# Packed attention, gated MLP and routed attention, eight sequences: keys and queries turned head by head between matrix products, GpSimd joins the planes, last queries' scores block-diagonal

## The chip, the cores and the metric

One core of a Trainium2 chip runs the whole program. The metric is device time in microseconds (us) of one execution, the median of several. "TensorE" is PE (PEld is its weight load), "VectorE" DVE, "ScalarE" ACT, "GpSimd" POOL; SyncE (SP) only issues DMAs.

## What is computed

For each of 8 sequences (b = 0 to 7) of 576 tokens, three layers follow one another:

```
p_packed = softmax(p k^T / 8) v                 # 8 heads of 64, 32 packed queries per head
x        = softmax(q p_packed^T / 8) p_packed   # back to 576 tokens, 512 wide
h = gelu(x w_in);  u, v = halves of h;  v = layernorm(v) * g
x = x + (u * (w_sg v + b_sg)) w_out             # mixing over tokens
# four experts, each a causal attention over the whole sequence with a head of 64
out = sum over the two best experts e of gate_e(x) * softmax(x wq_e (x wk_e)^T / 8, causal) x wv_e wo_e
```

Products are float32; most are made from a high and a low part of each operand in three passes (`PASSES`).

## The kernel before

**Stages of a sequence.** TensorE's order is written out by hand (`manual_schedule`). `startup` prepares the weights (w_in and w_out arrive as float64 bit patterns and are rebuilt on VectorE) and does sequence 0 as far as its gated product; its last steps load `moe2_wo` into `wst` (`prep_w_o`, L311) and split it into `w_o`. Then comes `back(0)`, and for b = 1 to 7 `front(b)` and `back(b)`. `front` makes the v part of the MLP (`v_tiles`) and the u part (`u_tile`). `back` mixes the tokens (`vs_tile`), makes the per-head products `bdq` and `bdv` (`bdw`), then queries, keys, values and gate logits of the experts (`qk`, `vlog`, `gates`). Between these stand the expert attention of sequence b-1 (steps S, T, y, o: scores and softmax, transposes, product with the values, output) and the packed attention of sequence b+1. A **loop** below is the time from the start of `v_tiles` of one sequence to that of the next.

**Keys and queries of the packed attention** need the 64 head dims on partitions. From sequence 1 on, a DMA does that, on 16-bit halves. `turn` (L386) transposes two heads at once from the input into an SBUF tile `x` (two buffers), and writes the tile to a scratch tensor in DRAM (`turned_k`, `turned_q`). `planes` (L393) reads it back so that low and high half-words of a number stand in separate planes (`kp`, `qp`), and `join` (L399) interleaves the planes into float32 (`kT`, `qT`): plane 0 is copied on GpSimd, plane 1 on ScalarE. Step K joins keys (K0 two pairs of heads, K1 two) and loads query planes, Q joins queries; s0 and s1 are the scores of the packed queries with the keys (L436), a0 and a1 transpose the softmax (L463, from the exponentials of L445), p and P make the packed values, r the second softmax. Step f, in `back` after the last `vs_tile`, loads the key planes of the next sequence and half of its values.

**The last queries.** Tokens 512 to 575 are a tile of 64 rows. For a pair of experts, `att_last` (L884; steps S8 and S9) makes 12 products of 64x64 by 288 into two PSUM tiles, one per expert (L896), adds the mask (L902), takes the maximum (L903) and the exponential (L904) of each, and scales both (L905 to L907). PSUM has four tiles (`pd`).

**Order.** Only TensorE's order is the program's. For ACT, DVE, POOL and SP a list scheduler with a model of times sets the order; each engine then executes in order, and SP issues its DMAs in order, each with its own waits (buffers, data). `ahead(b)` adds the load of p and the eight turns for sequence b; `startup` calls `ahead(1)`, and `back(b)` calls `ahead(b+2)`. kept_qk, kept_vg, kept_in are weights rearranged in DRAM, of which `load_w` brings w_qk, w_vg and the halves of w_in each time into two buffers (tag W).

Of the kernel before, what the change touches and what calls it, by code (L numbers as in the profile page):

```python
# [7 lines left out]
F32 = mybir.dt.float32  # L8
# [9 lines left out]
P = 128  # L18
# [8 lines left out]
def packed_attention_mlp_moe_kernel(  # L27
# [37 lines left out]
    BY = {"A": 1152, "B": 576, "C": 640, "D": 576, "a": 1152, "p": 576, "T": 512, "x": 576, "t": 576, "W": 2048}  # L65
# [33 lines left out]
    for i in range(E):  # L99
        for j in range(E):  # L100
            nc.vector.memset(tri[:, i, j:j + 1], 1.0 if j < i else 0.0)
    mhalf = consts.tile([P, 1], F32, name="mhalf")
# [219 lines left out]
    def load_nat(name, src, b, j):  # L322
# [6 lines left out]
        elif (b, name) == (0, "k") and j >= 2:  # L329
            t = slot("x", w=512, name=name)  # L330
        else:
            t = nat_slot(F32, name)
# [27 lines left out]
    STEP = {}  # L360

    def p1_steps(b):
# [23 lines left out]
        def turn(name, src, j):  # L386
            x = sb.tile([P, 2, S], U16, tag="x", name=name + "x", bufs=NB["x"])
            rows = src[b, 2 * j:2 * j + 2].rearrange("h s d -> (h s) d").bitcast(U16)
            nc.sync.dma_start_transpose(x.rearrange("p h s -> p (h s)"), rows)
            s[name + "x", j] = dram.tile([P, 2, S], U16, name=f"turned_{name}{b}{j}")  # L390
            nc.sync.dma_start(s[name + "x", j], x)
# [7 lines left out]
        def join(name, j):  # L399
# [3 lines left out]
            nc.gpsimd.tensor_copy(w[:, 0], t[:, 0].rearrange("p h n -> p (h n)"))  # L403
            act_copy(w[:, 1], t[:, 1].rearrange("p h n -> p (h n)"))
# [141 lines left out]

        for name, src in (("k", k), ("q", q)):
            for j in range(4):
                add(0, turn, name, src, j)
# [249 lines left out]

    def vlog(b, cs):  # L800
# [83 lines left out]
    def att_last(b, pr):  # L884

        s = ST[b]
        qs, ks = s["qk", pr], s["qk", 2 + pr]
        at = slot("B" if b + 1 == B else "a", w=S, name="at")
        st = small.tile([P, 2, 2], F32, name="st3")
        sm = small.tile([P, 2], F32, name="sm4")  # L890
        pts = [pd("sc") for _ in range(2)]
        for i, (x, y) in enumerate(PASSES):
            for h in range(2):
                for e in range(2):
                    r = slice(64 * e, 64 * e + 64)
                    nc.tensor.matmul(pts[e][:64, h, :HALF], qs[x][r, 4 * P:S], ks[y][r, hs(h)],  # L896
                                     start=i == 0, stop=i == 2)
        for e in range(2):
            r = slice(64 * e, 64 * e + 64)
            se = st[:64, e, :]  # L900
            d = pts[e][:64, 1, HALF - 64:HALF]
            nc.vector.tensor_tensor(d, d, causal[:64, :64], op=OP.add)  # L902
# [331 lines left out]
```

## Time and profile before

| | |
|---|---|
| Median of 3 runs | 960.96 us (960.46 to 961.58) |
| The profiled execution | 959.91 us, span 958.2 us (1.7 us lie outside) |
| PE busy | 839.3 us (88% of the span), 7613 products |
| DVE, ACT, POOL busy | 581.2, 477.2, 128.2 us |
| DMA | 114.09 MB, mean 119 GB/s |
| v_tiles of sequences 1, 2, 3, 7 start at | 202.8, 327.6, 428.4, 830.4 us |

How to read it: the engines run side by side, so a busy time counts only where something waits for it. A matmul's end is modelled. "[19.96 <-ACT u]" behind a row is the idle time of that engine before the instruction, and what ended it by the profile; where the named engine had long been done, it was something else, often a DMA. The chain that ended last is PE for 60% of the span, DMA for 9% and ACT for 6%.

### The profile page before, as it was taken

How to read it: one execution, taken by the hardware profiler on the slowest of the kernel's cores; microseconds unless marked ns; L12 is line 12 of the kernel's file. 1: busy time of each engine (PE TensorE's matmuls, PEld its weight loads, DVE VectorE, ACT ScalarE, POOL GpSimd, SP SyncE). 2: the span in 40 equal slices, each digit the busy share in tenths (PEclk: the TensorE clock that was granted, in tenths of full speed). 3: DMA queues.
4: the chain of work that ended last, by engine and by line, in shares of the span. 5: the costliest groups of instructions: out<-in, count | busy, mean ns of one | idle time of the engine just before them, and what ended most of it. 6: DMA issues, size and time to landing. Idle time of an engine off the chain costs nothing.

```text
span 958.2 us, 19292 instructions
## 1 busy us (share of the span) xinstructions
PE 839.3 (88%) x7613; PEld 701.8 (73%) x7613; DVE 581.2 (61%) x1419; ACT 477.2 (50%) x1061; POOL 128.2 (13%) x148
## 2 busy tenths in 40 slices
PE   4687634799577999899999999999999999999987
PEld 2457523688456897789878887888788877898965
DVE  7669241386333876478647765586548665876365
ACT  2445133265343566546563657275646565565345
POOL 0001030120011211021012101130112021210000
PEclk9898867899878999999999999999999999999989
DMA  9987889898794106320532144112422052200001
GB/s 302 249 216 172 196 236 254 207 197 203 213 260 104 68 1 201 85 72 3 169 94 56 43 134 116 45 68 72 151 71 67 25 172 64 68 1 35 12 7 50
DMA packets 168870, 114.09 MB, mean 119 GB/s; under 512 B 115594, under 2 KB 149642, under 8 KB 165964
## 3 DMA queue, kind: packets, MB, share of 16 engines
q1 hardware_dynamic: 168780, 112.86, 43.4%
q8 instruction: 60, 0.98, 0.4%
q14 instruction: 30, 0.25, 0.1%
HBM read 68.26 MB, written 29.63 MB: 102 GB/s over the span
## 4 chain that ended last, share of the span: by engine, by line
PE 60%; DMA 9%; ACT 6%; DVE 4%; issue 2%; SPq 1%; ACTq 0%
PE qk L774 9%; PE vs L729 8%; PE vlog L811 5%; PE qk L786 5%; PE v L661 4%; PE y L951 4%; PE u L711 4%; PE o L982 4%; PE sc L864 4%; PE vlog L815 3%; DMA qx<-in_q_dram 2%; PE aTp L922 2%; DMA turned_q<-qx 2%; DMA kx<-in_k_dram 2%; ACT at L904 1%
## 5 line engine op out<-in xcount | busy, mean ns | idle before, releaser
L774 PE MATMUL qk<-gh,w_qk 128*128 128x288 f32 x512 | 91.9, 302 | 2.2 <-ACT at L904 2.1
L729 PE MATMUL vs<-w_sg,vnh 128*128 128x288 f32 x512 | 92.8, 304 | 0.7 <-DVE w_sg L85 0.7
L774 PEld LDWEIGHTS qk<-gh,w_qk 128*128 128x128 f32 x512 | 75.2, 190 | 14.9 <-issue 7.2
L82 ACT ACTIVATE aT<-aTp 128x512 f32<-128x512 f32 (+4 forms) x160 | 60.5, 433 | 46.8 <-PE aTp L922 41.7
L877 ACT ACTIVATE at<-sc,nm 128x256 f32<-128x256 f32 (+3 forms) x128 | 66.4, 525 | 27.2 <-DVE nm L868 27.1
L729 PEld LDWEIGHTS vs<-w_sg,vnh 128*128 128x128 f32 x512 | 75.7, 191 | 5.3 <-issue 3.0
L982 PE MATMUL o<-w_o,y 128*128 128x512 f32 x192 | 55.8, 428 | 12.4 <-ACT pT L82 11.0
L811 PE MATMUL vlog<-w_vg,gh 128*128 128x260 f32 (+1 forms) x320 | 61.9, 291 | 0.0
L951 PE MATMUL y<-aT,v 128*64 128x128 f32 (+2 forms) x960 | 60.3, 265 | 0.8 <-ACT aT L82 0.8
L676 POOL TENSOR_TENSOR rstd<-rstd,mhalf 128x1 f32<-128x1 f32 x40 | 36.9, 929 | 164.4 <-DVE rstd L675 164.4
L951 PEld LDWEIGHTS y<-aT,v 128*64 128x64 f32 (+1 forms) x960 | 47.7, 138 | 13.9 <-issue 7.0
L774 PE MATMUL qk<-gl,w_qk 128*128 128x288 f32 x256 | 55.4, 298 | 1.9 <-DVE gl L85 1.9
L403 POOL COPY kT<-kp 128x576 uint16<-128x576 uint16 x28 | 24.8, 913 | 237.0 <-DMA kp<-turned_k 164.6
L729 PE MATMUL vs<-w_sg,vnl 128*128 128x288 f32 x256 | 55.4, 298 | 0.0
L868 DVE TENSOR_REDUCE nm<-sc 128x2 f32<-128x256 f32 (+3 forms) x64 | 52.6, 822 | 1.6
L881 DVE TENSOR_SCALAR at<-at,sm,gw 128x256 f32<-128x256 f32 (+3 forms) x128 | 51.4, 443 | 2.3
L982 PEld LDWEIGHTS o<-w_o,y 128*128 128x128 f32 x192 | 35.7, 200 | 23.3 <-ACT pT L82 11.2
L811 PEld LDWEIGHTS vlog<-w_vg,gh 128*128 128x128 f32 (+1 forms) x320 | 48.2, 180 | 3.5 <-issue 2.8
L864 PE MATMUL sc<-qk 64*128 64x256 f32 (+3 forms) x384 | 47.9, 356 | 0.0
L922 PE MATMUL aTp<-ident,at 128*128 128x128 f32 x320 | 47.8, 282 | 0.0
L786 PE MATMUL qk<-a2h,bdq 128*128 128x288 f32 x256 | 46.6, 303 | 0.2 <-DVE bdq L85 0.2
L878 DVE TENSOR_SCALAR sm<-sm 128x2 f32<-128x2 f32 x64 | 14.0, 218 | 52.5 <-ACT at L877 52.4
(208 smaller groups left out, 1947.7 us busy)
## 6 DMA issues: line engine op xcount, KB each, us to landing
w_in<-kept_in SPq DMA_DIRECT2D x14, 1024.0 KB
w_qk<-kept_qk SPq DMA_DIRECT2D x8, 1024.0 KB
out_dram<-ot SPq DMA_DIRECT2D x32, 256.0 KB
turned_k<-kx SPq DMA_DIRECT2D x28, 288.0 KB
turned_q<-qx SPq DMA_DIRECT2D x28, 288.0 KB
kp<-turned_k SPq DMA_DIRECT2D x56, 144.0 KB
qp<-turned_q SPq DMA_DIRECT2D x56, 144.0 KB
v<-in_v_dram SPq DMA_DIRECT2D x56, 128.0 KB
```

Source lines behind the costliest of these rows:

```text
L82: nc.scalar.activation(o, i, AF.Copy, scale=scale)
L729: nc.tensor.matmul(pt[:, h, :HALF], s["vn", c][x][:, cols], w_sg[y][:, c, hs(h)], start=(c, x, y) == (0, 0, 0), stop=False)
L774: nc.tensor.matmul(o[:, h, :], W["w_qk"][y][:, m, cols], s["g", m][x][:, hs(h)], start=first and (m, x, y) == (0, 0, 0), stop=not first an ...
L786: nc.tensor.matmul(o[:, h, :], s["bd", Q][y][:, cols], s["a2", Q][x][:, hs(h)], start=first and (Q, x, y) == (0, 0, 0), stop=not first and ...
L811: nc.tensor.matmul(pt[:n, ci, :260], s["g", m][x][:, c * P:c * P + n], W["w_vg"][y][:, m, :], start=(m, x, y) == (0, 0, 0), stop=False)
L864: nc.tensor.matmul(pt[:, e, :L], qs[x][r, j * P:L], ks[y][r, :L], start=i == 0, stop=i == 2)
L868: nc.vector.tensor_reduce(nm, pt[:, :, :L], axis=AX.X, op=OP.max, negate=True)
L877: nc.scalar.activation(ats[e][:, :L], pt[:, e, :L], AF.Exp, bias=nm[:, e:e + 1], accum_out=sm[:, e:e + 1])
L881: nc.vector.tensor_scalar(ats[e][:, :L], ats[e][:, :L], sm[:, e:e + 1], s["w"][:, j, 2 * pr + e:2 * pr + e + 1], op0=OP.mult, op1=OP.mult)
L922: nc.tensor.transpose(pt[:, e, c * P:c * P + P], ats[e][:, c * P:c * P + P], ident)
L951: nc.tensor.matmul(pt[64 * e:64 * e + 64, pr * w:pr * w + w], s["v2"][:m, c, col:col + D], s["aT", pr, e, j][c][:m, :], start=c == 0, stop ...
L982: nc.tensor.matmul(pt, ys[:, pr, x, :], W["w_o"][y][:, pr, :], start=i == 0, stop=i == 5)
```

## The change

- `turn` transposes one head, with one buffer of half the size; `keep` writes it to DRAM as a DMA of its own, in the next step. These steps stand in a list (`TURN`, 17 per sequence: 16 turns, each behind the `keep` of the head before, and a last `keep`). `tick` takes the next one: ten in `front(b)`, the rest before step f, six in `back(b)` for the sequence after; all 17 of sequence 1 at the end of `startup`.
- SP executes in program order from `back(0)` on.
- `join` makes both copies on GpSimd.
- `keep_last_q` copies the last 64 queries of a pair of experts (high and low part) into the diagonal blocks of a 128x128 tile of zeros, on GpSimd. `att_last` makes 6 products of 128x128 by 288 into one PSUM tile, and one maximum and one exponential over 128 partitions.
- S8 moves ahead of T6, S9 ahead of T7; step f ahead of "T5 S6 o1 T4".

```diff
@@ pools, constants, load_nat
-    BY = {"A": 1152, "B": 576, "C": 640, "D": 576, "a": 1152, "p": 576, "T": 512, "x": 576, "t": 576, "W": 2048}
+    BY = {"A": 1152, "B": 576, "C": 640, "D": 576, "a": 1152, "p": 576, "T": 512, "t": 576, "W": 2048}
+    last_q = [[consts.tile([P, P], F32R, name=f"last_q{i}{x}") for x in range(2)] for i in range(2)]
+    for z in last_q[0] + last_q[1]:
+        nc.gpsimd.memset(z.bitcast(F32), 0.0)
...
         elif (b, name) == (0, "k") and j >= 2:
-            t = slot("x", w=512, name=name)
+            t = slot("D", w=512, name=name)
@@ p1_steps
+    TURN = []
+
+    def tick(n=1):
+        for _ in range(min(n, len(TURN))):
+            for f in TURN.pop(0):
+                f()
...
-        def turn(name, src, j):
-            x = sb.tile([P, 2, S], U16, tag="x", name=name + "x", bufs=NB["x"])
-            rows = src[b, 2 * j:2 * j + 2].rearrange("h s d -> (h s) d").bitcast(U16)
-            nc.sync.dma_start_transpose(x.rearrange("p h s -> p (h s)"), rows)
-            s[name + "x", j] = dram.tile([P, 2, S], U16, name=f"turned_{name}{b}{j}")
-            nc.sync.dma_start(s[name + "x", j], x)
+        def turn(name, src, h):
+            x = sb.tile([P, S], U16, tag="x", name=name + "x", bufs=NB["x"])
+            nc.sync.dma_start_transpose(x, src[b, h].bitcast(U16))
+            if h % 2 == 0:
+                s[name + "x", h // 2] = dram.tile([P, 2, S], U16, name=f"turned_{name}{b}{h}")
+            s["x", name, h] = x
+
+        def keep(name, h):
+            nc.sync.dma_start(s[name + "x", h // 2][:, h % 2, :], s.pop(("x", name, h)))
...
-            nc.gpsimd.tensor_copy(w[:, 0], t[:, 0].rearrange("p h n -> p (h n)"))
-            act_copy(w[:, 1], t[:, 1].rearrange("p h n -> p (h n)"))
+            for i in range(2):
+                nc.gpsimd.tensor_copy(w[:, i], t[:, i].rearrange("p h n -> p (h n)"))
...
+        last = None
         for name, src in (("k", k), ("q", q)):
-            for j in range(4):
-                add(0, turn, name, src, j)
+            for h in range(H):
+                TURN.append([lambda a=last: a and keep(*a), lambda a=(name, src, h): turn(*a)])
+                last = (name, h)
+        TURN.append([lambda a=last: keep(*a)])
@@ attention
+    def keep_last_q(b, pr):
+        for z, t in zip(last_q[pr], ST[b]["qk", pr]):
+            for e in range(2):
+                r = slice(64 * e, 64 * e + 64)
+                nc.gpsimd.tensor_copy(z[r, r], t[r, 4 * P:S])
...
-        st = small.tile([P, 2, 2], F32, name="st3")
+        st = small.tile([P, 2], F32, name="st3")
-        pts = [pd("sc") for _ in range(2)]
+        pt = pd("sc")[:, :, :HALF]
         for i, (x, y) in enumerate(PASSES):
             for h in range(2):
-                for e in range(2):
-                    r = slice(64 * e, 64 * e + 64)
-                    nc.tensor.matmul(pts[e][:64, h, :HALF], qs[x][r, 4 * P:S], ks[y][r, hs(h)],
-                                     start=i == 0, stop=i == 2)
+                nc.tensor.matmul(pt[:, h, :], last_q[pr][x], ks[y][:, hs(h)], start=i == 0, stop=i == 2)
         for e in range(2):
             r = slice(64 * e, 64 * e + 64)
-            se = st[:64, e, :]
-            d = pts[e][:64, 1, HALF - 64:HALF]
-            nc.vector.tensor_tensor(d, d, causal[:64, :64], op=OP.add)
-            nc.vector.tensor_reduce(se[:, 0:1], pts[e][:64, :, :HALF], axis=AX.XY, op=OP.max, negate=True)
-            nc.scalar.activation(two(at[r, :]), pts[e][:64, :, :HALF], AF.Exp, bias=se[:, 0:1], accum_out=se[:, 1:2])
-            nc.vector.tensor_scalar(sm[r, 0:1], se[:, 1:2], EPS, None, op0=OP.add)
+            d = pt[r, 1, HALF - 64:]
+            nc.vector.tensor_tensor(d, d, causal[r, r], op=OP.add)
+        nc.vector.tensor_reduce(st[:, 0:1], pt, axis=AX.XY, op=OP.max, negate=True)
+        nc.scalar.activation(two(at), pt, AF.Exp, bias=st[:, 0:1], accum_out=st[:, 1:2])
+        nc.vector.tensor_scalar(sm[:, 0:1], st[:, 1:2], EPS, None, op0=OP.add)
@@ front, back, startup, schedule
-        v_tiles(b, VT[0])
-        v_tiles(b, VT[1])
-        v_tiles(b, VT[2])
+        for cs in VT:
+            v_tiles(b, cs)
+            tick(2)
         u_tile(b, 0)
         go("T0")
+        tick()
         for m in range(1, 4):
             u_tile(b, m)
+            tick()
...
-            go("T5 S6 o1 T4")
+        tick(len(TURN))
         if b + 1 < B:
             STEP.pop((b + 1, "f"))()
+        go("T5 S6 o1 T4")
...
-        do_all("K0 T6 o2 S8 s0 T7")
+        do_all("K0 S8 T6 o2 s0 S9 T7")
+        keep_last_q(b, 0)
...
-            do_all("y3 S9 a0 K1 s1 Q0 p0 T8 o3 a1 T9 Q1")
+            do_all("y3 a0 K1 s1 Q0 p0 T8 o3 a1 T9 Q1")
...
             vlog(b, VT[0])
+            tick()
         vlog(b, VT[1])
+        tick()
...
         qk(b, 1)
+        keep_last_q(b, 1)
+        tick()
         nxt("S0" if b + 1 < B else "S8")
+        tick()
         qk_packed(b, 3, True)
         nxt("S2" if b + 1 < B else "S6")
+        tick()
...
         qk_gated(b, 3, False)
+        tick()
...
-        ahead(1)
         keep_w_all()
...
         weights(0, ("qk", "vg"))
+        ahead(1)
+        tick(len(TURN))
         for m in range(4):
             u_tile(0, m)
...
-    with tc.manual_schedule(engines={mybir.EngineType.PE}):
+    with tc.manual_schedule(engines={ET.PE, ET.SP}):
```

**SP at the end of startup.** Rows from the last turns to the load of `moe2_wo` (`wst`), before:

```order
L389 DMA_TRANSPOSE qx<-in_q_dram 128x1152 x2
L391 DMA turned_q_1528<-qx 128x1152
L397 DMA kp<-turned_k_451 64x4x288 x2
L397 DMA kp<-turned_k_455 64x4x288 x2
L397 DMA kp<-turned_k_459 64x4x288 x2
L196 DMA kept_in_103<-w_in 128x512 x2
L397 DMA kp<-turned_k_463 64x4x288 x2
L391 DMA turned_q_1532<-qx 128x1152
L389 DMA_TRANSPOSE kx<-in_k_dram 128x1152
L196 DMA kept_in_103<-w_in 128x512 x2
L315 DMA wst_1103<-in_moe_wo_dram 128x512
```

and in the changed kernel:

```order
L397 DMA_TRANSPOSE qx<-in_q_dram 128x576 x2
L403 DMA turned_q_1052<-qx 128x576 x2
L409 DMA kp<-turned_k_1003 64x4x288 x2
L409 DMA kp<-turned_k_1010 64x4x288 x2
L409 DMA kp<-turned_k_1017 64x4x288 x2
L199 DMA kept_in_111<-w_in 128x512 x2
L409 DMA kp<-turned_k_1024 64x4x288 x2
L199 DMA kept_in_111<-w_in 128x512
L318 DMA wst_1135<-in_moe_wo_dram 128x512
```

Before, the turns ahead of `wst` are those of sequence 2 (the q pair shown) and the first of sequence 3, and sequence 1 had its own much earlier, among the weight copies; now they are sequence 1's 16 turns, behind 20 weight copies (kept_qk, kept_vg), and no other sequence is turned before `back(0)`.

**POOL and PE in a later `back`.** POOL from one sequence's `rstd` to its second softmax, before and (second block) changed; `last_q` is the tile of the last queries:

```order
L676 TENSOR_TENSOR rstd<-rstd,mhalf 128x1 x5
L403 COPY kT<-kp 128x576 x4
L403 COPY qT<-qp 128x576 x4
L513 TENSOR_TENSOR bt<-bt,mx_2813 128x576
L513 TENSOR_TENSOR bt<-bt,mx_2842 128x576
```

```order
L691 TENSOR_TENSOR rstd<-rstd,mhalf 128x1 x5
L416 COPY kT<-kp 128x576 x4
L819 COPY last_q_94<-qk 64x64 x2
L819 COPY last_q_95<-qk 64x64 x2
L416 COPY kT<-kp 128x576 x4
L416 COPY qT<-qp 128x576 x8
L525 TENSOR_TENSOR bt<-bt,mx_2861 128x576
```

The joins double on POOL and are gone from ACT; the copies of the last queries stand between the joins of K0 and K1. On PE, from the transposes of p to those of step T7, changed:

```order
L390 MATMUL pT<-ident,pn 128x128 x2
L915 MATMUL sc<-qk,last_q_94 128x288 x4
L915 MATMUL sc<-qk,last_q_95 128x288 x2
L939 MATMUL aTp<-ident,at 128x128 x8
...
L448 MATMUL s_2518<-kT,pT 32x288 x8
L915 MATMUL sc<-qk,last_q_96 128x288 x4
L915 MATMUL sc<-qk,last_q_97 128x288 x2
L939 MATMUL aTp<-ident,at 128x128 x8
```

Before, the 12 products of S8 stood behind the output product (in the place of "..."), right ahead of s0, and those of S9 after the next `qk` and y3.

**ACT at the end of startup**, changed: the first copy of `w_o` stands ahead of `wph`, the part of the weights that the products of u need; before, both copies stood behind it.

```order
L82 ACTIVATE vs<-vs 128x576
L82 ACTIVATE w_o_1133<-wst_1135 128x512
L642 ACTIVATE wph<-wp 128x1024
L82 ACTIVATE w_o_1133<-wst_1139 128x512
L729 ACTIVATE u<-u 128x576
```

## Rows read from the trace of the kernel before

**Rows 1.** The page, busy tenths in 40 slices of 24 us: TensorE and DMA.
```profile
PE   4687634799577999899999999999999999999987
DMA  9987889898794106320532144112422052200001
```

**Rows 2.** Stretches: length, busy us (instructions) of PE, PEld, DVE, ACT, POOL; clock; DMA.
```profile
111.60:202.80 91.20, 49.89 (x489) 39.08 (x487) 33.75 (x78) 27.63 (x52) 17.12 (x16) 0.78 0.89 222
202.80:327.60 124.80, 102.21 (x937) 85.93 (x932) 66.19 (x164) 56.83 (x125) 16.86 (x19) 0.89 0.71 182
428.40:528.40 100.00, 97.50 (x931) 82.87 (x931) 66.49 (x164) 56.33 (x125) 16.79 (x19) 1.00 0.29 87
830.40:958.20 127.80, 118.86 (x984) 101.17 (x984) 74.52 (x189) 66.51 (x165) 4.62 (x5) 0.97 0.07 24
```

**Rows 3.** Timeline of SP's queue, 39 to 127 us: start, us, issue, [idle before].
```profile
39.80 2.12 SPq L389 DMA_TRANSPOSE kx<-in_k_dram  x1
...
44.13 3.27 SPq L140 DMA_DIRECT2D raw_in<-in_moe_w_in_dram  x5
...
91.21 5.37 SPq L389 DMA_TRANSPOSE kx<-in_k_dram  x2
...
116.51 3.88 SPq L397 DMA_DIRECT2D kp<-turned_k  x6
...
126.06 1.45 SPq L315 DMA_DIRECT2D wst<-in_moe_wo_dram  x2
```

**Rows 4.** Timeline of ACT, 130 to 172 us.
```profile
130.41 1.26 ACT L82 ACTIVATE w_o<-wst 128x512 fp32r<-128x512 f32 x2 [27.04 <-DMA wst<-in_moe_wo_dram]
...
171.36 0.84 ACT L82 ACTIVATE qT<-qp 128x576 uint16<-128x576 uint16 x1 [12.79 <-DMA qp<-turned_q]
```

**Rows 5.** Timeline of PE, 103 to 174 us.
```profile
103.42 0.80 PE L711 MATMUL u<-a2h,wph 128*128 128x288 f32 x4 [1.24 <-ACT wph L627]
...
132.27 1.96 PE L610 MATMUL bdq<-w_qk,ppT 64*32 64x512 f32 x16 [19.96 <-ACT u L714]
...
145.87 1.93 PE L436 MATMUL s<-kT,pT 64*32 64x288 f32 x16 [1.57 <-issue]
...
172.93 1.11 PE L463 MATMUL a1T<-ident,a 128*128 128x128 f32 x4 [15.49 <-ACT a L445]
```

**Rows 6.** Waits of PE, 202.8 to 327.6 us: in total, times, longest.
```profile
PE o L982 <- ACT pT L82: 11.0, 1, 11.0
```

**Rows 7.** The chain that ended last, 210 to 253 us: start, us, what.
```profile
210.58 8.23 DMA qx<-in_q_dram
...
247.17 3.17 DMA qx<-in_q_dram
...
250.35 2.16 DMA turned_q<-qx
```

**Rows 8.** Waits of PE, 428.4 to 528.4 us.
```profile
PE aTp L936 <- ACT at L904: 0.7, 1, 0.7
```

**Rows 9.** Timeline of SP's queue, 428 to 467 us.
```profile
428.48 0.34 SPq L184 DMA_DIRECT2D w_vg<-kept_vg  x1
...
461.63 5.13 SPq L397 DMA_DIRECT2D kp<-turned_k  x8
```

**Rows 10.** Timelines of POOL and PE: the first join and the scores after it.
```profile
465.37 0.85 POOL L403 COPY kT<-kp 128x576 uint16<-128x576 uint16 x1 [23.17 <-DMA kp<-turned_k]
...
480.99 0.72 PE L436 MATMUL s<-kT,pT 64*32 64x288 f32 x16
```

**Rows 11.** Timelines of POOL and DVE, 134 to 139 us: joins beside VectorE work.
```profile
134.09 5.12 POOL L403 COPY kT<-kp 128x576 uint16<-128x576 uint16 x4
...
134.68 2.59 DVE L747 TENSOR_TENSOR vs<-vs,u 128x576 f32<-128x576 f32 x2
```

**Rows 12.** Timeline of PE: last queries' scores, and 24 full-array products (chain).
```profile
480.05 1.01 PE L896 MATMUL sc<-qk 64*64 64x288 f32 x12
...
415.37 3.19 PE qk L774 x24
```

More of the change, by code (lines that the diff above doesn't have):

```diff
@@ L886, in att_last @@
         s = ST[b]
-        qs, ks = s["qk", pr], s["qk", 2 + pr]
+        ks = s["qk", 2 + pr]
         at = slot("B" if b + 1 == B else "a", w=S, name="at")
-        st = small.tile([P, 2, 2], F32, name="st3")
+        st = small.tile([P, 2], F32, name="st3")
         sm = small.tile([P, 2], F32, name="sm4")
-        pts = [pd("sc") for _ in range(2)]
+        pt = pd("sc")[:, :, :HALF]
         for i, (x, y) in enumerate(PASSES):
             for h in range(2):
-                for e in range(2):
-                    r = slice(64 * e, 64 * e + 64)
-                    nc.tensor.matmul(pts[e][:64, h, :HALF], qs[x][r, 4 * P:S], ks[y][r, hs(h)],
-                                     start=i == 0, stop=i == 2)
+                nc.tensor.matmul(pt[:, h, :], last_q[pr][x], ks[y][:, hs(h)], start=i == 0, stop=i == 2)
         for e in range(2):
             r = slice(64 * e, 64 * e + 64)
-            se = st[:64, e, :]
-            d = pts[e][:64, 1, HALF - 64:HALF]
-            nc.vector.tensor_tensor(d, d, causal[:64, :64], op=OP.add)
-            nc.vector.tensor_reduce(se[:, 0:1], pts[e][:64, :, :HALF], axis=AX.XY, op=OP.max, negate=True)
-            nc.scalar.activation(two(at[r, :]), pts[e][:64, :, :HALF], AF.Exp, bias=se[:, 0:1], accum_out=se[:, 1:2])
-            nc.vector.tensor_scalar(sm[r, 0:1], se[:, 1:2], EPS, None, op0=OP.add)
+            d = pt[r, 1, HALF - 64:]
[3 more added lines that the diff above has]
+        nc.vector.tensor_scalar(sm[:, 0:1], st[:, 1:2], EPS, None, op0=OP.add)
         nc.vector.reciprocal(sm[:, 1:2], sm[:, 0:1])
@@ L1058, in back @@
         qk_out(b, 0)
-        do_all("K0 T6 o2 S8 s0 T7")
+        do_all("K0 S8 T6 o2 s0 S9 T7")
+        keep_last_q(b, 0)
         qk(b, 2)
         if b + 1 == B:
-            go("y3 S9 T8 o3")
+            go("y3 T8 o3")
             vlog(b, VT[2])
```

## The prediction

> **What bounds the kernel now.** I read the page's slices first, then stretches, then what each queue did where TensorE stood still.
>
> The slices [rows 1] part the run in three. To about 110 us weights are rebuilt. From there to 300 us DMA is at 7 to 9 tenths, PE swings between 3 and 9. After that PE is at 9 and DMA at 1 to 4.
>
> The stretches [rows 2] give sizes. A late loop, 428.4 to 528.4, is 100.0 us with PE busy 97.5: PE bounds it. Loop 1, 202.8 to 327.6, does the same work (937 products against 931) in 124.8 us. `back(0)`, from the end of its u products at 111.6, takes 91.2 us with PE busy 49.9 and a clock of 0.78. Both have DMA at 0.71 to 0.89, a late loop 0.29.
>
> The reason is in SP's queue [rows 3]: sequence 1 is turned from 39.8 us, sequence 2 from 91.2, then all the others, one after another, until DMA falls off near 300 us [rows 1]. What is wanted soon stands behind them, and each engine waits in its order. The load of `wst` is issued at 126.06; ACT has waited 27.04 us for it [rows 4], with the activations of u behind, so `bdq` starts 19.96 us late [rows 5]. ACT then stands 12.79 us at a join whose plane has not come [rows 4], and the exponential behind it holds the transposes a1 up by 15.49 us [rows 5]. In loop 1 it happens again, 11.0 us with the copy of pT behind a join [rows 6]. In a late loop PE idles 100.0 - 97.5 = 2.5 us, some of it at the exponentials of S9 [rows 8].
>
> **The change, part by part.** The sum is made against the profiled execution, 959.91 us; the median is 1.05 above it.
>
> *A, startup.* The turns of sequence 1 now stand behind 31 issues (20 weight copies, 4 kept_in, 5 raw_in, p twice) at about 0.65 us (3.27 for five) [rows 3], 20 us in all, and begin near 58 us: the copies start two issues ahead of the 39.8 of the first turn today. What 16 turns of one head cost is not in the trace. Today four pairs of two-head turns with their writes take 25.3 us (91.21 to 116.51) [rows 3], 6.3 a pair; one such turn lands after 3.17 us, a write after 2.16 [rows 7]. A pair of half-size turns costs at least half, 25 us for all eight, and, with no gain from size, the same, 51. I take 4.5 a pair, 36 us, since a landing hardly shrinks while issue and packets halve. Then 4 us for w_qk and w_vg among them, 5 us for the key planes (5.13 for eight) [rows 9] and a write or two, and `wst` is issued near 105 and lands near 109 (today 126.06 and 130.41: 4.35 later). Behind it come one copy, `wph` and u, now in that order: u starts near 111 (today 103.42), lasts 8.2, and `bdq` starts near 119.5 instead of 132.27. s0, 13.6 us after it today, keeps about 12.5 of that: the activations of u run along with PE now, but four joins on POOL take 3.4 us in a row. s0 at 132 instead of 145.87: **14 us won**. With turns at 25 or 51 us it is 25 or 0.
> The Trainium skill (DMA: Bandwidth & Descriptors, Anatomy of one DMA) counts a fixed 2.0 us for every DMA whatever its size, measured on GpSimd's queue, and so speaks against halving them. By that, an estimate: 16 more DMAs, two in flight at a time, add 16 us to the half of 25.3; the turns take 41 us, A is 9 and the forecast 897. The writes' 2.16 us agree with it; no row here has a turn of one head.
>
> *B, the rest of back(0).* No join stands on ACT, so the wait of 15.49 goes but for the exponential itself: **15 us**. Late next are the second values and query planes, needed 6 us later; I allow nothing more.
>
> *C, loop 1.* Sequences 3 to 7 are no longer turned there. It becomes a late loop, below: 124.8 - 98.5 = **26.3 us**; 20 if some wait stays.
>
> *D, the five late loops* (502.8 us together from 327.6 to 830.4, 100.6 each). An `att_last` is 12 products in 1.01 us; six full-array ones at 3.19 / 24 = 0.133 us are 0.80 [rows 12]: 0.4 us a loop. The tiles are also softened once and earlier (S9 a whole `qk` earlier), ACT loses eight joins, and of 2.5 us of waits I leave 0.5. A loop is 98.2: **12 us**.
> The Trainium skill (TensorEngine Tiling (Array Packing), Tiling Modes) lets 64-row tiles work at the same time, which speaks against a matrix half of zeros: 12 such products would take no longer than six full ones, and the 0.4 would be 0; these rows, 1.01 against an estimated 0.80, show the overlap incomplete.
>
> *E, the tail*, 127.8 us [rows 2]: two `att_last` and shorter softmaxes, **1.5 us**, by their share of D.
>
> *Costed at nothing.* The 14 to 17 ticks of a loop: SP has nothing else between w_vg and the key planes, 33 us [rows 9], and DMA is at 0.29; eight sequences' worth of turns only moves. The 8 copies of last queries a loop fall between joins; at 64 elements to a plane's 576 they take at most a join's 0.85 us each, and are wanted a loop later. The extra POOL joins (8 a loop at 0.85, 6.8 us [rows 10]) lie in time that POOL waits; the first four end 1.7 us later than two and two did, while s0 follows the first join's start by 15.6 us [rows 10].
>
> Sum: 14 + 15 + 26.3 + 12 + 1.5 = 68.8, so 891.1 for a profiled execution and 892 for the median. With the low ends (A 25, C 27, D 14, E 3) it is near 877; with the poor ones (A 0, B 12, C 20, D 0, E 0) near 929.
>
> **The rivals.**
>
> *Turns still in front of wst.* For: A rests on a price the trace lacks, and if 16 turns need 51 us, `wst` lands at 124 and ACT now has `wph` behind it. Against: they are half as large and alone in the queue. A is 0: 906.
>
> *Planes late, the slower end.* SP now executes in order, and a tick is serial: the write waits for the turn before, the next turn for a free buffer. Ten ticks stand between w_vg at 0.1 us of a loop and the key planes. Planes start 33.2 us into the loop today and s0 is at 52.6; from the issue of the first planes to the first join are 3.7 us [rows 9, 10] and four joins need 3.4, so the planes may start at 45 without harm: up to 4.4 us a tick. Beyond that s0 waits ten times the excess in six loops; 68.8 us are used up at 56, a tick of 5.6. At 6 us a tick the planes start at 60, and it is 892 + 6 x 15 = 982. For: a turn took 8.23 us beside a load of w_qk [rows 7], which is again ahead of the ten. Against: the others there took 3.17, which with 0.34 for the write's issue is 3.5 a tick, at twice the size. A tick of 5 us would give 922.
>
> *Joins that slow VectorE.* Four joins beside VectorE took 5.12 us, 1.28 each instead of 0.85 [rows 10], and two VectorE products in that time 2.59 [rows 11]. The joins of a loop are 16, so if every one met VectorE work on the path, 16 x 0.43 = 7 us in six loops would be lost: 933; half of it 912. Against: VectorE is busy 66% of a loop and PE is the bound.
>
> *The change does not do it:* SP is held by an output or a buffer in its new order so that planes come as late as now. Then A to D shrink to nothing: 958 to 962.
>
> **How the numbers follow.** Forecast as above, 877 to 908: 0.66. Turns in front of wst, or a like loss in startup: 0.10. VectorE slowed: 0.10. Planes somewhat late, 909 to 940: 0.06; late to the point of a loss: 0.05. No effect: 0.03. The first four are faster by far more than 0.2% (2 us, about what a measurement of this kernel can tell from no change): 0.92. Of no effect I count 0.02 as within it and 0.01 as slower: slower 0.06. The range takes the forecast's ends and most of the next three: 874 to 926.
>
> **What would show it.** `wst` issued near 105 and `bdq` near 120 (A); no wait of a1 or of pT's copy over 2 us (B, C); loops of 98 to 99 from the first on, DMA near 0.5 throughout instead of 0.9 then 0.3; PE waits below 1 us a loop, and none at S8 or S9 (D). Against it: PE waiting at L448 (s0) for joins, kT waiting for kp late in the loop; `turned` writes with long waits on SP; a v_tiles of sequence 1 later than 190 us.

## The result and the profile after

The changed kernel takes **893.24 us** (median of 4 runs, 890.41 to 895.45) against 960.71 for the kernel before (4 runs on the same chip, 959.80 to 961.58): a ratio of **0.9296, 95% interval 0.9265 to 0.9327**. The profiled execution took 891.95 us, its span is 890.2. The forecast was 892.

The page's slices of the changed kernel, now of 22 us each, show the shape the forecast drew. Against [rows 1] the swing of PE up to 300 us is gone, and DMA, before at 7 to 9 up to some 290 us and at 0 to 6 from there on, is spread over the run.

```profile
PE   3587777999999999999999999999999999999987
DMA  9886654346635393446625573538344650200001
```

The stretches that answer to [rows 2], in the same columns: `back(0)` from 111.6 on, loop 1, a late loop, the tail.

```profile
111.60:178.96 67.36, 54.78 (x530) 46.54 (x530) 32.79 (x78) 22.55 (x45) 22.15 (x32) 0.87 0.45 130
178.96:276.54 97.58, 96.83 (x927) 82.87 (x919) 67.15 (x161) 49.31 (x113) 25.80 (x35) 1.00 0.52 133
471.64:568.87 97.23, 96.54 (x926) 82.91 (x919) 66.94 (x160) 49.30 (x113) 25.74 (x35) 1.00 0.52 136
763.60:890.20 126.60, 118.62 (x968) 101.68 (x960) 73.11 (x182) 63.03 (x157) 6.47 (x13) 0.97 0.07 24
```

Loop 1 is now a loop like the others. The span fell by 68.0 us: sequence 1 starts 23.8 us sooner (178.96 for 202.8), loop 1 is 27.2 shorter, the five late loops together 15.8 (487.06 for 502.83), the tail 1.2.

The start, in SyncE's queue (start, us, issue), answers to [rows 3]: the turns of sequence 1 run from 60.11 to the last write behind 102.74, then come the key planes, then `wst`.

```profile
60.11 2.54 SPq L397 DMA_TRANSPOSE kx<-in_k_dram  x2
...
102.74 1.92 SPq L403 DMA_DIRECT2D turned_q<-qx  x2
104.75 3.87 SPq L409 DMA_DIRECT2D kp<-turned_k  x6
...
111.75 0.42 SPq L318 DMA_DIRECT2D wst<-in_moe_wo_dram  x1
```

Who waits for it now, on ScalarE and then on TensorE [rows 4, 5]:

```profile
115.77 0.63 ACT L82 ACTIVATE w_o<-wst 128x512 fp32r<-128x512 f32 x1 [10.82 <-DMA wst<-in_moe_wo_dram]
116.31 1.00 ACT L642 ACTIVATE wph<-wp 128x1024 fp32r<-128x1024 f32 x1
```
```profile
117.36 1.33 PE L726 MATMUL u<-a2h,wph 128*128 128x288 f32 x4 [12.14 <-ACT wph L642]
...
126.40 1.09 PE L625 MATMUL bdq<-w_qk,ppT 64*32 64x512 f32 x16
...
135.47 0.68 PE L448 MATMUL s<-kT,pT 64*32 64x288 f32 x4 [2.34 <-POOL kT L416]
136.95 1.20 PE L448 MATMUL s<-kT,pT 64*32 64x288 f32 x12 [0.81 <-POOL kT L416]
...
148.79 0.66 PE L475 MATMUL a1T<-ident,a 128*128 128x128 f32 x4 [1.24 <-ACT a L457]
```

The wait for `wst` has become shorter, 10.82 us for 27.04, and has moved: ScalarE's copy of `w_o` now stands ahead of `wph`, and u waits 12.14 us where `bdq` waited 19.96. The 15.49 us of a1T are 1.24, little more than the 0.93 that the exponential and the reading of its sum take on ScalarE. The scores wait for the joins, for a reason that GpSimd's timeline shows: the joins of keys stand behind the first copy of the last queries, which waits for the products of qk.

```profile
133.66 0.23 POOL L819 CAST last_q<-qk 64x64 fp32r<-64x64 f32 x1 [14.48 <-ACT qk L809]
133.86 3.04 POOL L416 COPY kT<-kp 128x576 uint16<-128x576 uint16 x4
```

In a late loop, from 471.64, most ticks on SyncE's queue are 2.8 to 3.1 us from write to write; three are longer, the first, beside w_qk, with 4.47. The key planes are issued at 505.36, 33.7 us into the loop (33.2 in [rows 9]), and PE waits for two things only, 0.7 us together; the waits of [rows 8] for the exponential are gone.

```profile
472.65 1.13 SPq L397 DMA_TRANSPOSE kx<-in_k_dram  x1
476.64 0.32 SPq L403 DMA_DIRECT2D turned_k<-kx  x1
...
486.56 1.13 SPq L397 DMA_TRANSPOSE qx<-in_q_dram  x1
489.20 0.32 SPq L403 DMA_DIRECT2D turned_q<-qx  x1
...
505.36 5.15 SPq L409 DMA_DIRECT2D kp<-turned_k  x8
```
```profile
PE pp L490 <- DVE a1t L477: 0.4, 1, 0.4
PE s L448 <- ACT ppT L509: 0.3, 1, 0.3
```

### The profile page after: what moved, and what is told of

It is laid out like the page before. It is cut to its first block, busy times and chain, and to the rows that moved or that the text cites. A ratio compares the mean times of both kernels' runs of the same rounds, so it can differ in the third digit from the quotient of the medians.

```text
span 890.2 us, 19164 instructions
## 1 busy us (share of the span) xinstructions
PE 827.7 (93%) x7517; PEld 699.4 (79%) x7517; DVE 582.1 (65%) x1387; ACT 424.7 (48%) x973; POOL 188.5 (21%) x272
## 4 chain that ended last, share of the span: by engine, by line
PE 80%; DVE 6%; DMA 5%; ACT 3%; issue 3%; SPq 2%; POOL 0%; ACTq 0%; POOLq 0%; DVEq 0%
PE vs L744 12%; PE qk L789 10%; PE y L968 6%; PE vlog L832 6%; PE v L676 6%; PE qk L801 5%; PE o L999 5%; PE u L726 5%; PE sc L885 4%; PE aTp L939 4%; PE vlog L836 3%; DMA raw_in<-in_moe_w_in_dram 2%; PE fold L300 2%; PE sc L915 2%; PE wp L625 2%
## 5 line engine op out<-in xcount | busy, mean ns | idle before, releaser
L416 POOL COPY kT<-kp 128x576 uint16<-128x576 uint16 x56 | 48.1, 924 | 149.1 <-DMA kp<-turned_k 100.3
L691 POOL TENSOR_TENSOR rstd<-rstd,mhalf 128x1 f32<-128x1 f32 x40 | 36.9, 927 | 161.8 <-DVE rstd L690 161.8
L902 DVE TENSOR_SCALAR at<-at,sm,gw 128x256 f32<-128x256 f32 (+3 forms) x128 | 60.4, 514 | 2.3
L968 PEld LDWEIGHTS y<-aT,v 128*64 128x64 f32 (+1 forms) x960 | 48.4, 140 | 14.1 <-issue 7.3
L999 PE MATMUL o<-w_o,y 128*128 128x512 f32 x192 | 52.4, 408 | 0.5 <-ACT y L978 0.5
L819 POOL CAST last_q<-qk 64x64 fp32r<-64x64 f32 x64 | 14.9, 233 | 178.1 <-PE sc L915 85.5
L416 POOL COPY qT<-qp 128x576 uint16<-128x576 uint16 x56 | 44.7, 873 | 11.8 <-DMA qp<-turned_q 11.8
```

The lines of the kernel that those rows point to most:

```text
L416: nc.gpsimd.tensor_copy(w[:, i], t[:, i].rearrange("p h n -> p (h n)"))
L902: nc.vector.tensor_scalar(ats[e][:, :L], ats[e][:, :L], sm[:, e:e + 1], s["w"][:, j, 2 * pr + e:2 * pr + e + 1], op0=OP.mult, op1=OP.mult)
L968: nc.tensor.matmul(pt[64 * e:64 * e + 64, pr * w:pr * w + w], s["v2"][:m, c, col:col + D], s["aT", pr, e, j][c][:m, :], start=c == 0, stop ...
L999: nc.tensor.matmul(pt, ys[:, pr, x, :], W["w_o"][y][:, pr, :], start=i == 0, stop=i == 5)
```

## The experiments

Twelve kernels in three sets, each beside the kernel before on the same chip. The table has the stages of each profiled execution: when sequence 1's v_tiles start, the length of loop 1, the mean of the five loops behind it, the tail, the span, all in us; then the median of all runs and its ratio to before. The ratio goes by the kernel before in the same set, whose medians were 962.03, 957.30 and 960.57 us (960.71 beside the changed kernel), so medians of different sets compare to some 4 us only, and ratios and stages better. A stage is one execution's: late loops of the same kernel differ by up to 1 us, and by more where the clock falls in one.

| kernel | sequence 1 | loop 1 | late loop | tail | span | median | ratio [95%] |
|---|---|---|---|---|---|---|---|
| before | 202.8 | 124.8 | 100.6 | 127.8 | 958.2 | 960.71 | 1 |
| changed | 179.0 | 97.6 | 97.4 | 126.6 | 890.2 | 893.24 | 0.9296 [0.9265, 0.9327] |
| order_alone | 180.2 | 100.1 | 100.3 | 126.4 | 908.1 | 911.96 | 0.9477 [0.9429, 0.9524] |
| join_alone | 218.4 | 111.6 | 99.7 | 128.3 | 956.8 | 957.99 | 0.9957 [0.9933, 0.9981] |
| join_act | 179.3 | 99.8 | 99.1 | 126.3 | 900.9 | 902.37 | 0.9379 [0.9334, 0.9425] |
| att_old | 176.3 | 99.6 | 100.0 | 127.7 | 903.6 | 905.44 | 0.9403 [0.9353, 0.9453] |
| att_late | 179.9 | 99.0 | 99.0 | 126.4 | 900.4 | 902.07 | 0.9387 [0.9347, 0.9427] |
| sp_free | 218.2 | 137.2 | 99.1 | 127.1 | 978.0 | 978.54 | 1.0211 [1.0175, 1.0246] |
| x1 | 191.2 | 103.7 | 110.2 | 126.2 | 972.1 | 973.87 | 1.0180 [1.0134, 1.0225] |
| pairs_old | 171.2 | 99.7 | 99.7 | 128.8 | 898.3 | 899.24 | 0.9356 [0.9309, 0.9403] |
| wst_early | 175.6 | 97.6 | 97.2 | 125.7 | 885.0 | 885.95 | 0.9246 [0.9215, 0.9277] |
| last_dve | 174.4 | 98.8 | 98.9 | 126.3 | 894.0 | 896.75 | 0.9361 [0.9329, 0.9392] |
| wo_pool | 166.8 | 97.4 | 97.5 | 126.3 | 877.9 | 879.90 | 0.9156 [0.9117, 0.9194] |
| best | 168.5 | 98.2 | 97.4 | 126.7 | 880.2 | 879.26 | 0.9154 [0.9113, 0.9196] |

### Which part won what

**order_alone**: the change without its joins and without its attention of the last queries. It is the change's diff without these pieces:

```diff
-            for i in range(2):
-                nc.gpsimd.tensor_copy(w[:, i], t[:, i].rearrange("p h n -> p (h n)"))
+            nc.gpsimd.tensor_copy(w[:, 0], t[:, 0].rearrange("p h n -> p (h n)"))
+            act_copy(w[:, 1], t[:, 1].rearrange("p h n -> p (h n)"))
...
-                nc.tensor.matmul(pt[:, h, :], last_q[pr][x], ks[y][:, hs(h)], start=i == 0, stop=i == 2)
+                for e in range(2):
+                    r = slice(64 * e, 64 * e + 64)
+                    nc.tensor.matmul(pts[e][:64, h, :HALF], qs[x][r, 4 * P:S], ks[y][r, hs(h)],
...
-        do_all("K0 S8 T6 o2 s0 S9 T7")
+        do_all("K0 T6 o2 S8 s0 T7")
```

> The kernel before, with the turns head by head in program order and the startup's turns behind the weights, but with plane 1 still joined on ScalarE and the old attention of the last queries. Theory (order frees the start and loop 1, joins free the wait inside the startup, the attention gives the late loops): the start's 9 to 10 us to s0 and most of loop 1's 27 us come back, ScalarE then finds its planes on time and waits for none, so loop 1 takes 100 to 102 us, the five late loops stay at 100 to 101 us each; total 908 to 922 us. Rival (the joins are what blocks, the order only shifts the wait): loop 1 stays above 112 us and the total above 935 us.

911.96 us, as the theory had it: 50 of the 68 us come with the turns head by head in program order (0.0523 of 960.7). Sequence 1 starts within 1.3 us of the changed kernel's, loop 1 falls from 124.8 to 100.1, and the late loops stay at 100.3. In the startup the a1 transposes still wait 4.87 us for the exponential behind ScalarE's joins; that is all that is left of the 15.49.

**join_alone**: the kernel before, both planes joined on GpSimd.

```diff
-            nc.gpsimd.tensor_copy(w[:, 0], t[:, 0].rearrange("p h n -> p (h n)"))
-            act_copy(w[:, 1], t[:, 1].rearrange("p h n -> p (h n)"))
+            for i in range(2):
+                nc.gpsimd.tensor_copy(w[:, i], t[:, i].rearrange("p h n -> p (h n)"))
```

> The kernel before with one edit: both planes are joined on GpSimd. Theory: ScalarE is no longer blocked (the waits of PE for a1T, 15.5 us in the startup, and for pT, 11.0 us in loop 1, shrink to under 3 us each), but the planes still land late behind the turns, so PE waits for the joined keys and queries instead; 5 to 20 us come back, total 940 to 956 us. Rival (the blocked ScalarE was the whole of it): 25 us or more come back, total under 935 us.

957.99 us, 0.4% less than before: 4 us came back where the theory had 5 to 20, and the rival 25 or more. The waits went as expected, but others took their place. PE's waits up to sequence 1 (total, times, longest):

```profile
PE pp L478 <- DMA v<-in_v_dram: 27.7, 2, 27.1
PE bdq L610 <- ACT u L714: 18.7, 1, 18.7
...
PE a1T L463 <- ACT a L445: 1.2, 1, 1.2
```

a1T waits 1.2 us, not 15.5. The values that pp needs are now issued at 184.91, behind turns of a later sequence, where the kernel before had them at 171.32: the scheduler's order of SyncE's queue had shifted with the one edit. So the startup lost 15.6 us while loop 1 won 13.2. The edit is therefore not a clean price of the joins; what it shows is that in this run freeing ScalarE only handed the wait on.

**join_act**: the changed kernel with the two lines of the join put back (the first piece of the diff under order_alone).

> The changed kernel with plane 1 joined on ScalarE again. Theory: with planes that land on time the engine of the join hardly matters in the loops; 1 to 5 us of the startup (its queries' planes) come back as a wait for ScalarE; total 893 to 900 us, each late loop within 0.6 us of the changed kernel's 97.2 to 97.9. Rival (the joins carry about 15 us of their own): total 905 to 910 us.

902.37 us: neither. The startup hardly moved (179.3 for 179.0), but each late loop took 99.1 us on average, 1.7 more, one of them 101.0. PE's waits in that one:

```profile
PE a1T L475 <- ACT a L457: 1.9, 1, 1.9
```

Even with planes on time ScalarE's eight joins of a loop (54.5 us busy for 49.3) put the exponentials a little later, and PE feels it. In that loop the granted clock also fell to half of full speed (1.2 GHz) from 743.0 to 746.4 us; the other four take 98.6 on average, so the joins are worth 1.2 us a loop without it. The theory that the engine of the join does not matter in the loops falls. From order_alone to att_old the same move wins only 0.3 us a loop, no more than such loops scatter, so the joins seem to pay more once the attention's waits are gone.

**att_old** and **att_late**: the changed kernel with the old `att_last` and the old places of S8 and S9; and with the new `att_last` in the old places. The second as a diff (the first also puts the old `att_last` back, with the matmul piece above, and has no copies of last queries):

```diff
-        do_all("K0 S8 T6 o2 s0 S9 T7")
+        do_all("K0 T6 o2 S8 s0 T7")
...
-            do_all("y3 a0 K1 s1 Q0 p0 T8 o3 a1 T9 Q1")
+            do_all("y3 S9 a0 K1 s1 Q0 p0 T8 o3 a1 T9 Q1")
```

> The changed kernel with the old attention of the last queries (24 matmuls on half the rows in place of 6 full ones per pair) and its two steps at their old places. Theory: PE's busy time per loop goes up by 1.0 us and its waits by 1.5 to 2.5 us, each late loop takes 99.7 to 100.8 us as before the change, and the total is 908 to 914 us. Rival (the late loops gained from the order of SP, not from the attention): late loops stay under 98.5 us, total 893 to 900 us.

> The changed kernel with the block-diagonal attention of the last queries, but its two steps at their old places. Theory (2.4 us a loop came from 1.0 us less of PE's work and 1.4 us of waits, and the waits are cured by the earlier places): late loops 98.2 to 99.2 us, total 896 to 906 us. Rival (fewer small steps on VectorE and ScalarE cure the waits, the places do nothing): late loops 97.2 to 97.9 us, total 889 to 896 us.

att_old took 905.44 us with late loops of 100.0, below the total expected, since its startup is 2.7 us shorter than the changed kernel's: no copies of last queries stand ahead of the joins, and its clock stays at full speed from 126 us on (more under last_dve). att_late took 902.07 with late loops of 99.0, inside what the theory had. So of the 2.6 us a loop (100.0 to 97.4) 1.0 comes from the block-diagonal form and 1.6 from the two steps being earlier. The waits of PE in a loop of att_old, and in one of att_late:

```profile
PE pp L487 <- ACT at L916: 1.2, 1, 1.2
PE qk L786 <- ACT at L916: 0.4, 1, 0.4
```
```profile
PE a1T L475 <- ACT a L457: 0.9, 1, 0.9
```

In att_old PE waits for the exponential of the last queries; in att_late that is gone, and the exponential of the next block, behind it on ScalarE, is late. Each is cured by one of the two edits. Neither pp nor qk reads that exponential's output: by the program they need a PSUM tile, and at pp all four are taken, two by S9 and the others by a1T and s1. So the block-diagonal form may win by taking one tile instead of two as much as by its fewer instructions on ScalarE (51.0 us busy in a loop of att_old, 49.2 in att_late); no run here parts the two.

**sp_free**: SyncE's queue left to the scheduler, everything else as changed.

```diff
-    with tc.manual_schedule(engines={ET.PE, ET.SP}):
+    with tc.manual_schedule(engines={ET.PE}):
```

> The changed kernel with SyncE's queue left to the scheduler again, while turns, joins and the attention of the last queries stay as changed. Theory (the order of the queue is what carries the start and loop 1): turns of the next sequence stand ahead of weights, values and planes again, sequence 1 starts at 190 to 205 us instead of 179, loop 1 takes 104 to 120 us, the late loops 97 to 98.5, total 915 to 945 us. Rival (turning head by head in the program's places is enough): total 890 to 900 us.

978.54 us, 2% longer than the kernel before (ratio 1.0175 to 1.0246) and worse than the theory allowed. One line is worth some 85 us. From loop 3 on the loops are 97.3 us, as changed; all of the loss lies ahead of them. SyncE's queue at 107 to 132 us, and PE's waits in loop 1:

```profile
107.49 2.43 SPq L397 DMA_TRANSPOSE kx<-in_k_dram  x2
110.05 1.47 SPq L403 DMA_DIRECT2D turned_k<-kx  x2
111.96 2.43 SPq L397 DMA_TRANSPOSE kx<-in_k_dram  x2
...
126.27 0.94 SPq L318 DMA_DIRECT2D wst<-in_moe_wo_dram  x2
...
131.71 2.17 SPq L341 DMA_DIRECT2D v<-in_v_dram  x4
```
```profile
PE pp L490 <- DMA v<-in_v_dram: 27.0, 2, 26.6
PE s L448 <- POOL kT L416: 7.7, 2, 7.2
```

The four turns from 107.49 are sequence 2's, taken as soon as a buffer was free, ahead of `wst` and of the values. This is the forecast's rival "the change does not do it", made by hand: the tick places in the program do nothing unless the queue keeps to them.

### The rival with planes that come late

**x1**: one buffer for turned heads, so that a turn waits for the write before it.

```diff
-"nat": 2, "x": 2, "t": 4,
+"nat": 2, "x": 1, "t": 4,
```

> The changed kernel with one buffer for the turned heads instead of two, so that each turn waits until the one before is written back. It prices the lateness that the prediction put as a rival. Theory: a turn and its write take 4.5 to 5 us instead of 2.9 to 3.1, the keys' planes are issued 50 to 58 us into a loop instead of 33.7, past the 45 us from which the scores wait for them; each loop grows by 5 to 14 us, total 930 to 985 us. Rival (a write of 144 KB is short enough to fit in a turn's own time): ticks under 3.8 us, total 893 to 905 us.

973.87 us, in the theory's range. A late loop that starts at 515.21: SyncE's queue, TensorE's waits for the joins, and the stretch, with the columns of [rows 2]:

```profile
520.94 0.43 SPq L187 DMA_DIRECT2D w_vg<-kept_vg  x1
...
571.47 5.15 SPq L409 DMA_DIRECT2D kp<-turned_k  x8
```
```profile
PE s L448 <- POOL kT L416: 9.6, 2, 9.3
```
```profile
515.21:626.01 110.80, 100.53 (x926) 85.38 (x918) 65.55 (x160) 49.31 (x113) 24.32 (x35) 0.94 0.44 121
```

Most ticks are 4.2 to 4.4 us, for 2.8 to 3.1, but the one beside w_qk takes 9.06, so the ten of this loop take 4.94 each on average (3.28 in the changed kernel's). And w_vg is issued 5.7 us into the loop instead of 0.2, since the ticks ahead of it are longer too. So the key planes are issued 56.3 us into the loop for 33.7, and the scores wait 9.6 us for the joins. From the prediction's bound (planes at 45 us are harmless, after that one for one) 56.3 gives 11.3, so the bound was about right. What was off is the price of a tick: the prediction started its ten ticks at 0.1 us however long they are, and had 922 in all for a tick of 5 us. This loop is 13.4 us longer than the changed kernel's mean, the five late ones 12.8 on average, more than the wait: behind it the granted clock was at half of full speed (1.2 GHz) from 571.0 to 584.6 us, where the six products of S8 took 1.81 us instead of 1.04.

### What was left in the startup

**pairs_old**: att_old with two heads to a turn, in the same places of the queue.

```diff
-        def turn(name, src, h):
-            x = sb.tile([P, S], U16, tag="x", name=name + "x", bufs=NB["x"])
-            nc.sync.dma_start_transpose(x, src[b, h].bitcast(U16))
+        def turn(name, src, j):
+            x = sb.tile([P, 2, S], U16, tag="x", name=name + "x", bufs=NB["x"])
+            rows = src[b, 2 * j:2 * j + 2].rearrange("h s d -> (h s) d").bitcast(U16)
+            nc.sync.dma_start_transpose(x.rearrange("p h s -> p (h s)"), rows)
...
-            for h in range(H):
+            for h in range(H // 2):
```

> The kernel with the old attention of the last queries (att_old, 905.4 us) with two heads to a turn, 8 ticks in place of 16, in the same places of the queue. It prices a turn by instruction and by byte. Theory (a turn's time is mostly per instruction: 1.13 us of issue at one head, 1.2 to 1.3 at two in the kernel before): the startup's turns take 26 to 34 us in place of 44.6, wst is issued at 93 to 101 us, sequence 1 starts 5 to 11 us earlier, loops unchanged at 99.7 to 100.7, total 894 to 901 us. Rival (per byte): turns 40 to 46 us, total 903 to 908 us.

SyncE's queue of att_old, and of pairs_old: the first turn, and the key planes behind the last write; then what the planes of pairs_old waited for.

```profile
59.20 2.53 SPq L394 DMA_TRANSPOSE kx<-in_k_dram  x2
...
106.85 3.86 SPq L406 DMA_DIRECT2D kp<-turned_k  x6
```
```profile
60.21 6.30 SPq L395 DMA_TRANSPOSE kx<-in_k_dram  x2
...
92.19 1.44 SPq L400 DMA_DIRECT2D turned_q<-qx  x2
99.65 3.86 SPq L406 DMA_DIRECT2D kp<-turned_k  x6
```
```profile
SPq L406 <- PE vs L741: 6.2, 1, 6.2
```

Sixteen turns of att_old take 47.6 us up to the end of the last write (106.75), eight of twice the size 33.4 (to 93.63), the two weight loads among them in both: inside the theory's 26 to 34. Eight turns and eight writes less save 14.1 us, 1.8 a turn with its write. But the key planes gain only 7.2 us, and `wst`, at 106.72, misses the theory's 93 to 101: the planes waited 6.2 us for the products vs, since they go into the ten buffers that those products read from (tag B). Sequence 1 starts 5.1 us sooner, as the theory had it. The total, 899.24, is in the theory's range too; by the ratios it is 4.5 us less than att_old's, within the two intervals. Halving the turns cost the startup, then; with the block-diagonal attention the paired form was not tried.

**wst_early**: `wst` loaded into slots of its own, its loads written ahead of the weight copies and the turns.

```diff
         for j in range(4):
             load_raw_in(0, j)
+        for j in range(2):
+            load_w_o(j)
         keep_w_all()
...
```

> The changed kernel with the second layer's output weights (wst) issued ahead of the startup's turns, into slots of their own. Theory (the startup's shortfall is that wst is still issued behind 44.6 us of turns; the u products wait 12.14 us for it): u starts at 104 to 107 us instead of 117.4, everything behind it moves with it, sequence 1 starts at 166 to 170 us, total 879 to 885 us. Rival (the turns are the bound themselves, since the keys' planes can only be issued at their end at 105 us): u comes earlier but the scores wait for the joined keys by as much, total 889 to 893 us.

885.95 us, 1 us above the theory's range, and not by its way: u starts at 113.69, not 104 to 107. The load was issued at 62.05; ScalarE's copy of it and TensorE behind it:

```profile
67.88 1.30 ACT L82 ACTIVATE w_o<-wst 128x512 fp32r<-128x512 f32 x2 [10.18 <-DMA wst<-in_moe_wo_dram]
```
```profile
71.06 5.42 PE L300 MATMUL fold<-fqk,woT 128*128 128x512 f32 x8 [9.81 <-ACT woT L82]
...
113.69 0.78 PE L731 MATMUL u<-a2h,wph 128*128 128x288 f32 x4 [1.24 <-ACT wph L647]
```

The copy of `w_o` now stood ahead of the copies of `woT`, and TensorE waited 9.81 us there (2.04 in the changed kernel); the 12.14 us in front of u were gone, but most of them had been spent. The span is 5.2 us shorter than the changed kernel's, and by the ratios the total 4.8. That led to another theory: not the load, but the copy in ScalarE's queue is the obstacle, wherever the load stands.

**wo_pool**: that copy made on GpSimd, and the load left where it was.

```diff
         hi, lo = W["w_o"]
-        act_copy(hi[:, j, :], st)
+        nc.gpsimd.tensor_copy(hi[:, j, :], st)
```

> The changed kernel with the rounding copy of the output weights (w_o, the one that waits for wst) made on GpSimd instead of ScalarE; the load stays behind the turns. Theory (u does not need w_o at all, it waited 12.14 us only because ScalarE's queue has the copy of w_o ahead of wph): u starts at 106 to 108 us instead of 117.4, the first scores at 124 to 128 instead of 135.5, sequence 1 at 167 to 171 us, total 880 to 886 us. Rival (GpSimd now waits for wst ahead of the joins and the scores wait for those): the first scores stay at 133 us or later, total 889 to 894 us.

**879.90 us**, better than both kernels: 13.3 less than the changed one, with u at 105.86, the first scores at 123.77 and sequence 1 at 166.8, each just past the better end of the theory.

```profile
105.86 0.80 PE L726 MATMUL u<-a2h,wph 128*128 128x288 f32 x4 [1.24 <-ACT wph L642]
...
123.77 0.68 PE L448 MATMUL s<-kT,pT 64*32 64x288 f32 x4 [2.35 <-POOL kT L416]
125.26 1.20 PE L448 MATMUL s<-kT,pT 64*32 64x288 f32 x12 [0.81 <-POOL kT L416]
```

**last_dve** and **best**: the copies of the last queries on VectorE, in all sequences of the changed kernel; and on VectorE in the first sequence alone, on top of wo_pool. The line of the second (the first has `nc.vector` alone):

```diff
-                nc.gpsimd.tensor_copy(z[r, r], t[r, 4 * P:S])
+                (nc.gpsimd if b else nc.vector).tensor_copy(z[r, r], t[r, 4 * P:S])
```

> The changed kernel with the eight copies per sequence into the block-diagonal queries made on VectorE instead of GpSimd. Theory (in the startup GpSimd stands 14.48 us at the first of these copies, ahead of the joins of keys whose planes have landed, and the scores wait 2.34 and 0.81 us for the joins): the scores of the startup start 3 us earlier, the loops stay within 0.4 us each, total 888 to 891 us. Rival (VectorE, 67 us busy in a loop of 97, delays the attention's maxima instead): loops 0.5 us longer each, total 892 to 897 us.

> The same, and the first sequence's copies of its last queries on VectorE (the other sequences' on GpSimd as changed). Theory (those copies held back the joins of the startup, 4.5 us to sequence 1, while on VectorE they cost each loop 1.4 us): 2 to 5 us more come off the startup and the loops keep 97.2 to 97.9 us each, total 876 to 883 us. Rival (both removed waits were the same one): no more than 1 us below the kernel with w_o on GpSimd alone.

last_dve won 4.6 us in the startup (174.4 for 179.0) and lost 1.5 in every loop (98.9 for 97.4): 896.75, the rival's outcome, at three times its size. Of the startup's gain the joins' wait is the smaller part, 2.2 us: the scores waited 0.9 us instead of 3.1. Behind that wait the changed kernel's granted clock was at half of full speed (1.2 GHz) from 136.2 to 143.0 us; in last_dve it stayed at full speed from 121.4 on. best took 879.26, no different from wo_pool: its rival holds. There GpSimd works on `w_o` until the products of qk are through anyway, so the joins begin at 122.58 without the copies and at 122.15 with them.

## Why the prediction was right

892 was forecast and 893.24 measured; the terms sum to 68.8 forecast against 68.0, of the span. The causes named for it (turns ahead of what is wanted, ScalarE behind a join) are what the runs show. That the total came within 1.2 us is in part luck: two terms were off, in opposite directions.

*A, startup: 14 us forecast, 8.9 measured* (from 145.87 to 136.95, where twelve of the first 16 scores start; the first four start at 135.47, which would be 10.4, and B 13.4). The mis-sized step is "I take 4.5 a pair, 36 us": with the 4 us for weight loads, 40 to the key planes, and 44.6 in the trace (60.11 to 104.75); the rest is that the turns began at 60.11, not near 58. `wst` was issued at 111.75 instead of 105 and u started at 117.36 instead of 111; part of it came back because the scores follow `bdq` by 9 to 10.5 us, not 12.5. The 3.17 and 2.16 us of [rows 7] on which the price leans were among the shortest of that stretch: the other turns there landed after 3.3 to 8.2 us, the other writes after 2.1 to 4.1. The page DMA: Bandwidth & Descriptors of the Trainium skill (Anatomy of one DMA) had it better: an estimate of 41 us (25.3 and 16) and the 4 make 45, and A 9. The trace agrees with that sum, and roughly with its 16: the 16 DMAs less of pairs_old saved 14.1 us against att_old. And the step took for granted that u needs `wst`; wo_pool shows that only ScalarE's order made it so, which was 13 us more.

*B, the rest of back(0): 15 us forecast, 14.9 measured* (from the first scores to sequence 1: 56.9 before, 42.0 after). order_alone has 9.8 of it (47.1) with the joins still on ScalarE: planes on time did more for the a1 wait than another engine.

*C, loop 1: 26.3 forecast, 27.2 measured*, and order_alone alone has 24.7 of them. Not all of it is waits: TensorE was idle 22.6 us of loop 1 before and 0.75 after, and the other 5.4 are busy time (102.21 and 96.83), at a granted clock of 0.89 before [rows 2] and 1.00 after. The forecast had this right because it set the loop equal to a late one; no term of the sum names the clock.

*D, the late loops: 12 forecast, 15.8 measured.* The size of the total came from another place than was said. "six full-array ones at 3.19 / 24 = 0.133 us are 0.80 [rows 12]: 0.4 us a loop" fell: the twelve occupied TensorE for 0.94 us to the next start [rows 10, 12], the six for 0.89.

```profile
520.94 1.04 PE L915 MATMUL sc<-qk,last_q 128*128 128x288 f32 x6
521.83 1.03 PE L939 MATMUL aTp<-ident,at 128*128 128x128 f32 x8
```

That is 0.05, or 0.1 a loop, so here too the Trainium skill's rule (TensorEngine Tiling (Array Packing), Tiling Modes), by which the saving would be 0, was nearer than my estimate from the chain. What the late loops won, 3.2 us each on average, is mostly waits. Of the 2.8 between the loops shown in [rows 2] and above, 1.8 are idle time (2.5 to 0.7, near the 0.5 forecast) and 1.0 busy time; of that the two products are 0.1, and where the rest lies is not shown, since a product's end is modelled and can reach into a wait. By edits the 3.2 are 0.3 from order_alone, as much again from the joins, then 1.0 from the block-diagonal form and 1.6 from the earlier places. The first 0.3 is no gain of the order: one loop before took 101.8 us, at a clock of 0.98, and the other four average 100.2 as order_alone's do.

*E, the tail: 1.5 forecast, 1.2 measured.*

*Costed at nothing.* The ticks held: 3.2 to 3.6 us on average in each loop, planes 33.4 to 36.9 us into it, under the bound of 45, and x1 shows what it would have cost otherwise, some 80 us in all. The copies of the last queries were not free in the startup (4.6 us there, by last_dve). That joins on GpSimd and VectorE slow each other was seen: the multiplication at L902 takes 514 ns for 443 at its line before, on average over its four shapes; the widest took 904 ns where a join of keys ran beside it and 542 elsewhere. The join of keys takes 924 ns on average for the 0.85 us of [rows 10]. The rival priced from that, 912 to 933, did not come about, since the loops are 97.4 us.

*The rival with turns still in front of wst* was half right: a wait of 12.14 us for it stood in the startup, but behind fewer us of turns than it needed to cost all 14.

## What to carry to other kernels

A queue that works in order is a schedule: one line that made SyncE keep to the program's places was worth some 85 us here, and neither smaller turns nor better-placed ones won anything without it. When an engine waits for a load, ask first whether the work behind it needs that load or only stands behind the copy of it: moving the copy to another engine gave 13 us, moving the load gave 5. When a kernel starts sooner, look at the clock as well as at the waits: here a wait of 3 us in the startup was followed by 6.8 us at half speed. Edits whose effects lie in waits do not add up; price them by taking each out of the finished kernel as well as by adding it to the old one.

## What the runs showed of the hardware that was not expected

A transposing load occupies the queue mostly by the instruction: 1.13 us for a head of 144 KB, 1.24 for two heads at once in pairs_old; with their writes, sixteen of one head took 47.6 us and eight of two 33.4. Six products of the full array with half of the weights zero take as long (0.89 us) as twelve of quarter tiles (0.94), so what the block-diagonal form wins is in the softmax's instructions, its PSUM tile and their waits, not on TensorE. And a short wait of TensorE was followed by a stretch at half clock more than once (x1, 9.3 us idle and 13.6 at 1.2 GHz in the loop shown; the changed kernel's startup, 3.1 and 6.8), so it cost more than its own length: 13.4 us in that loop for 9.6 of waiting.
